# Local attention in groups of 64 queries: 120 score columns a head, one transpose a head, one value product a group

## The chip, the core and the metric

The kernel runs on one core of a Trainium2 chip. A core has a matrix engine (TensorE, PE in the profile, with its weight loads listed apart as PEld), a vector engine (VectorE, DVE), a scalar engine (ScalarE, ACT), a general engine (GpSimd, POOL) and a queue that issues transfers (SyncE, SP). Each engine works through its own instructions in order. SBUF is the working memory with 128 partitions, PSUM the memory that TensorE writes, in eight banks. The metric is the device time of one execution in microseconds (us); lower is better.

## The reference, cut to what matters

Three layers follow each other: an attention, a feed-forward layer, and a mixture of eight experts. Only the attention is touched here. Its shapes are batch 2, 8 heads, 768 positions, 64 numbers a head, all in 32-bit floats:

```
block, window = (32, 16)                      # 24 blocks of 32 keys
k_sum = max of k over each block              # 24 summary keys a head
v_sum = mean of v over each block             # 24 summary values a head
scores_l = scale * q @ k.T, kept only where |query - key| < 16
scores_s = scale * q @ k_sum.T + log(32)
a = softmax over [scores_l, scores_s] together
out = a @ [v, v_sum]
```

So a query sees at most 31 near keys and 24 summary keys. After it come `h = x @ w_in`, `g = h * clip(h+3,0,6) / 6`, `g @ w_out`, the routing of tokens to experts with a cap of 192 each, and per expert `relu(x @ w1) @ w2`.

## The kernel before

Queries are taken in groups of 128 (12 groups `n`, six a batch). A group is worked in two halves `h` of four heads (two pairs `pr`), so the attention has 24 halves. For a half, `front` (L364) computes scores, `soften` (L391) the softmax, `turn` (L406) the transposed weights, and `values` (L416) the product with the values:

- `front`: for each head a matrix product with 64 contraction rows: the 128 queries are stationary (`qT`), and 184 columns move: 160 near keys (128 queries and 16 to each side) and 24 summary keys. `window` (L351) lays these keys out in the tile `kw`: one copy from `kT` (L360) and the summary keys twice (L361, L362), since even heads have the summaries behind the near keys and odd heads in front. Even heads lie on partitions 0 to 63 and odd heads on 64 to 127 of `qT` and `kw` (L371, L372). VectorE then adds the mask and takes the row maximum of each head (L381).
- `soften`: ScalarE takes the exponential with the sum of each row (L397); VectorE the reciprocal (L400); GpSimd multiplies the whole tile `A` (L402). `A` holds two heads in 384 columns, with 16 columns between them that are cleared at the start (L220).
- `turn`: a pair of heads is transposed in three pieces of 128 columns (L411), six a half, and ScalarE copies each pair out of PSUM (L413). The middle piece holds keys of both heads.
- `values`: `VA` holds 128 of the near values, `VB` what is left of them together with the summary values, for two heads side by side. Each head has a product with `VA` into its half of the PSUM partitions (L422, L423); each pair has one more with `VB`, added to it (L425). `load_v` (L163) brings the values with four transfers a group. `vsum_place` (L197) puts the mean values of a batch into `VB` (L203 by TensorE, L208 by VectorE), once a batch.

A matrix product in 32-bit floats is carried out as two matmuls, each with its weight load, so every such source line has twice as many instructions in the trace as in the code. A transpose is one.

The order of work on each engine is that in which the program is written. `drive` (L56) interleaves generators: each says with `yield` what its step is worth, and the one that is furthest behind its due time goes on. The numbers in these `yield`s and the due times (`ATTS`, `END`, `S0`, `S1`) are constants of the program. The first three groups of attention run in `prologue` (L735). The attention of the groups behind runs between the products of the first feed-forward layer, `gemm1` (L571: L581 to L583, twelve matmuls for each `f`, in 384 columns); its `gate` (L595) is on VectorE. Beside the first unit of `gemm1` the 64-bit-packed weights are still converted by VectorE (L275) and split by ScalarE and GpSimd (L292, L293). At most two halves are between `front` and `turn` (`LAG`).

Of the kernel before, what the change touches and what calls it, by code (L numbers as in the profile page):

```python
# [19 lines left out]
E, EF = 8, 1024  # L20
N = B * S
# [4 lines left out]
U = UT * 128  # L26
# [5 lines left out]
SCALE = 1.0 / math.sqrt(D)  # L32
NEG = -1e9 / SCALE
# [51 lines left out]
def build(ctx, tc, q, k, v, w_in, w_out, w_gate, w1, w2, out):  # L85
    nc = tc.nc
    PE, ACT, DVE, POOL, SP = nc.tensor, nc.scalar, nc.vector, nc.gpsimd, nc.sync
# [28 lines left out]
    def bank(i):  # L116
        return psum.tile([128, 512], FT, name=f"bank{i}")
# [3 lines left out]
    early = Arena()  # L121
    conv = Arena()
    sums = Arena()
    ident = consts.tile([128, 128], FT)
# [11 lines left out]
    mask = att.tile([128, 3, NB + 160 + NB], FT)  # L136
    LAG = 2
    Abuf = [att.tile([128, 2, 384], FT, name=f"A{i}") for i in range(LAG + 1)]
    VA = [att.tile([128, HP, 2, D], FT, name=f"VA{i}") for i in range(2)]
    VB = [att.tile([128, HP, 2 * D], FT, name=f"VB{i}") for i in range(2)]  # L140

    def warm(n):

# [17 lines left out]
        raw[kind, b, i] = x  # L161

    def load_v(n):  # L163
        b, i = divmod(n, 6)
        va, vb = VA[n % 2], VB[n % 2]
        i0 = i * 128
        for s in range(2):
            vh = v[b, s:H:2]
            lo = i0 - W if s == 0 else i0 + W
            a, z = max(lo, 0), min(lo + 128, S)  # L170
            SP.dma_start(va[a - lo:z - lo, :, s, :], vh[:, a:z, :].rearrange("h s d -> s h d"))
            lo, row = (i0 + 112, 0) if s == 0 else (i0 - W, 96)
            a, z = max(lo, 0), min(lo + 32, S)
            SP.dma_start(vb[row + a - lo:row + z - lo, :, s * D:(s + 1) * D],
                          vh[:, a:z, :].rearrange("h s d -> s h d"))
# [6 lines left out]
    zones, zi = flat[2][:, :192], flat[3][:, :192].bitcast(I32)  # L182

    def vsum(b, g):
        x, m = vss[g], BLK // 2
# [5 lines left out]
            m //= 2  # L191

    def zone():
        POOL.iota(zi, pattern=[[1, 192]], base=-48, channel_multiplier=-1)
        DVE.tensor_scalar(zones, zi, 0.0, 1.0 / BLK, op0=OP.is_equal, op1=OP.mult)

    def vsum_place(b):  # L197

        p = bank(4)
        for h in range(H):  # L200
            i, s = h % HP, h % 2
            at = 48 + NB * i - (32, 72)[s]
            PE.matmul(p[:, h * D:(h + 1) * D], zones[:, at:at + 128], vm[b][h // HP], start=True, stop=True)  # L203
        pv = p.rearrange("p (h s d) -> p h s d", s=2, d=D)
        for i in range(2):
            for s in range(2):
                r = slice(32 + 32 * s, 64 + 32 * s)
                DVE.tensor_copy(VB[i][r, :, s * D:(s + 1) * D], pv[r, :, s, :])  # L208

    raw["qraw", 0, 0] = q0[0]  # L210
    for g in range(2):
# [5 lines left out]
    for x in VA + VB:  # L217
        POOL.memset(x, 0.0)
    for x in Abuf:
        DVE.memset(x, 0.0)  # L220

    zone()
    band = early.take([160])
    POOL.iota(band, pattern=[[1, 160]], base=-W, channel_multiplier=-1,
              allow_small_or_imprecise_dtypes=True)
    DVE.tensor_tensor(band, band, band, op=OP.mult)
    DVE.memset(mask, math.log(BLK) / SCALE)
    for c in range(3):
        DVE.tensor_scalar(mask[:, c, NB:NB + 160], band, float(W * W), NEG, op0=OP.is_ge, op1=OP.mult)
    DVE.memset(mask[:, 0, NB:NB + W], NEG)  # L230
    DVE.memset(mask[:, 2, NB + 160 - W:NB + 160], NEG)


    WH, WL = {}, {}
# [102 lines left out]
    def q_prep(n, hps=range(HP)):  # L337
        b, i = divmod(n, 6)
        x = raw["qraw", b, i]
        p = bank(7 if n % 2 else 4)  # L340
        a, z = hps[0], hps[-1] + 1
        if a == 0:
            fr[n] = att.tile([128, HP, 128], FT, name="qT"), att.tile([128, HP, NB + 160 + NB], FT, name="kw")
        for hp in hps:
            PE.transpose(p[:, hp * 128:(hp + 1) * 128],
                         x[:, 2 * hp:2 * hp + 2, :].rearrange("p h d -> p (h d)"), ident)
        ACT.activation(fr[n][0][:, a:z], p[:, a * 128:z * 128].rearrange("p (h s) -> p h s", s=128), AF.Copy)
        if n >= UT and (n + 1) % 6:
            soon.append(partial(load_rows, "qraw", q, *divmod(n + 1, 6)))

    def window(n, hps=slice(0, HP)):  # L351
        i = n % 6
        kw = fr[n][1][:, hps]
        a, z = max(i * 128 - W, 0), min(i * 128 + 128 + W, S)
        c = NB + a - (i * 128 - W)
        if i == 0:
            DVE.memset(kw[:, :, NB:c], 0.0)
        if i == 5:
            DVE.memset(kw[:, :, c + z - a:NB + 160], 0.0)
        DVE.tensor_copy(kw[:, :, c:c + z - a], kT[:, hps, a:z])  # L360
        DVE.tensor_copy(kw[:, :, :NB], ks[:, hps])  # L361
        DVE.tensor_copy(kw[:, :, NB + 160:], ks[:, hps])  # L362

    def front(n, h, after):  # L364
        b, i = divmod(n, 6)
        qT, kw = fr[n]
        A = Abuf[(2 * n + h) % (LAG + 1)]
        sp = [bank(0), bank(1)]
        for pr in range(2):
            hp = 2 * h + pr  # L370
            PE.matmul(sp[0][:, pr * 192:pr * 192 + 184], qT[:64, hp, :], kw[:64, hp, NB:], start=True, stop=True)  # L371
            PE.matmul(sp[1][:, pr * 192:pr * 192 + 184], qT[64:, hp, :], kw[64:, hp, :NB + 160], start=True, stop=True)  # L372
        if after:
            q_prep(n + 1)
        mk = mask[:, 0 if i == 0 else 2 if i == 5 else 1]
        sm = att.tile([128, 4, 4], FT, name="sm", bufs=2)
        for pr in range(2):
            for s in range(2):
                o = A[:, pr, 0:184] if s == 0 else A[:, pr, 200:384]
                m = mk[:, NB:] if s == 0 else mk[:, :NB + 160]  # L380
                DVE.tensor_tensor_reduce(out=o, in0=sp[s][:, pr * 192:pr * 192 + 184], in1=m, scale=1.0,  # L381
                                         scalar=-3e38, op0=OP.add, op1=OP.max,
                                         accum_out=sm[:, 0, 2 * pr + s:2 * pr + s + 1])
        DVE.tensor_scalar(sm[:, 1], sm[:, 0], -SCALE, None, op0=OP.mult)
        if after:
            window(n + 1)
        later.append((A, sm))
# [2 lines left out]

    def soften():  # L391
        A, sm = later.pop()
        for pr in range(2):
            for s in range(2):
                o = A[:, pr, 0:184] if s == 0 else A[:, pr, 200:384]
                c = 2 * pr + s
                ACT.activation(o, o, AF.Exp, bias=sm[:, 1, c:c + 1], scale=SCALE, accum_out=sm[:, 2, c:c + 1])  # L397
        yield 1
        DVE.tensor_scalar(sm[:, 2], sm[:, 2], 1e-9, None, op0=OP.add)
        DVE.reciprocal(sm[:, 3], sm[:, 2])  # L400
        Av = A.rearrange("p a (s c) -> p (a s) c", s=2)
        POOL.tensor_tensor(Av, Av, sm[:, 3, :, None].to_broadcast([128, 4, 192]), op=OP.mult)  # L402

    ats = {}

    def turn(n, h):  # L406
        A = Abuf[(2 * n + h) % (LAG + 1)]
        for pr in range(2):
            p = bank(2 + pr)
            for c in range(3):  # L410
                PE.transpose(p[:, c * 128:(c + 1) * 128], A[:, pr, c * 128:(c + 1) * 128], ident)  # L411
            at = att.tile([128, U], FT, name="at", bufs=4)
            ACT.activation(at, p[:, :384], AF.Copy)  # L413
            ats[n, h, pr] = at

    def values(n, h):  # L416
        va, vb = VA[n % 2], VB[n % 2]
        if h == 0:
            xps[n] = bank(4 if n % 2 else 7)
        pair = [(2 * h + pr, ats.pop((n, h, pr)), xps[n][:, (2 * h + pr) * 128:(2 * h + pr + 1) * 128]) for pr in range(2)]  # L420
        for hp, at, o in pair:
            PE.matmul(o[:64], va[:, hp, 0, :], at[:, 0:128], start=hp == 0, stop=False, skip_group_check=True)  # L422
            PE.matmul(o[64:], va[:, hp, 1, :], at[:, 256:384], start=hp == 0, stop=False, skip_group_check=True)  # L423
        for hp, at, o in pair:
            PE.matmul(o, vb[:, hp, :], at[:, 128:256], start=False, stop=True, skip_group_check=True)  # L425
# [786 lines left out]
```

## Time and profile before

| what | value |
|---|---|
| median of 3 runs | 619.5 us (616.31 to 622.27) |
| the profiled execution's own time | 620.14 us |
| its span | 617.9 us |
| granted TensorE clock over the span | 0.981 |
| busy: TensorE, VectorE, ScalarE, GpSimd | 573.1, 413.6, 300.3, 191.0 us |
| TensorE's share of the span | 93% |
| bytes moved by transfers | 74.24 MB |

A row of the profile's list of groups reads: source line, engine, operation, what is written from what, the shape, the count, then the time in which at least one was busy, the mean of one in ns, and the idle time of the engine before it with what ended it. For a matmul, `128*64` is rows by columns of the stationary operand and `128x128` the moving one. The mean of a matmul is longer than the time from its start to the next start, because matmuls are pipelined: what one costs in a row of them is read from the starts in the timeline.

### The profile page before, as it was taken

Reading aid. Unit: us, or ns where it says so; the run is one execution under the profiler, and the core shown is the slowest. Engines: PE = TensorE matmul, PEld = TensorE weight load, DVE = VectorE, ACT = ScalarE, POOL = GpSimd, SP = SyncE. Lnnn points to the kernel's source line nnn. Section 1 sums busy time; section 2 is a strip of 40 time slices with the busy share of each in tenths; the row PEclk is TensorE's granted clock in tenths of the full one; section 3 lists DMA queues with packets and bytes.
Section 4 is the critical chain, followed back from the end, with each engine's and each line's share of the span. In section 5 each row is a group of like instructions: output and inputs, shape, how many; then the busy total and the mean of one; then the engine's idle time right before and its main releaser. Section 6 shows DMA issues by size and latency. Waiting matters only on the chain.

```text
span 617.9 us, 10534 instructions
## 1 busy us (share of the span) xinstructions
PE 573.1 (93%) x3571; PEld 483.5 (78%) x3571; DVE 413.6 (67%) x1197; ACT 300.3 (49%) x718; POOL 191.0 (31%) x212
## 2 busy tenths in 40 slices
PE   6688896999999998889999999999999999999993
PEld 5566775988889997776678787877788889888882
DVE  7878898454454338995003878876568888888880
ACT  3457654454555535554123213232656676767760
POOL 1535556610221104335235445435501011110111
PEclk8789999999999999999999999999999999999997
DMA  9945990211110024440006000000579889888910
GB/s 208 241 110 125 211 271 19 56 36 39 39 40 20 1 70 170 171 137 27 1 1 191 15 2 0 2 1 34 187 222 280 245 250 286 250 241 249 268 62 30
DMA packets 99710, 74.24 MB, mean 120 GB/s; under 512 B 44800, under 2 KB 85760, under 8 KB 99264
## 3 DMA queue, kind: packets, MB, share of 16 engines
q1 hardware_dynamic: 97664, 67.17, 39.3%
q0 software_dynamic: 1984, 6.32, 2.8%
q8 instruction: 30, 0.49, 0.3%
q14 instruction: 32, 0.26, 0.1%
HBM read 66.76 MB, written 6.71 MB: 119 GB/s over the span
## 4 chain that ended last, share of the span: by engine, by line
PE 48%; issue 26%; DVE 15%; POOL 5%; ACT 3%; DMA 2%; SPq 0%; POOLq 0%; ACTq 0%; DVEq 0%
PE bank L581 6%; PE bank L582 6%; PE bank L583 6%; PE bank L699 5%; DVE t L275 5%; PE bank L701 5%; PE bank L700 5%; POOL out_dram L1015 2%; PE bank L371 2%; PE bank L883 2%; POOL xs L630 2%; PE bank L608 2%; PE bank L411 2%; PE bank L425 2%; DVE A L381 1%
## 5 line engine op out<-in xcount | busy, mean ns | idle before, releaser
L581 PE MATMUL bank<-x,wh 128*128 128x384 f32 x256 | 92.4, 361 | 8.1 <-DVE t L596 8.1
L302 DVE TENSOR_TENSOR wl<-t,wh 128x1024 fp32r<-128x1024 f32 x64 | 77.0, 1221 | 20.4 <-ACT wh L301 16.9
L676 ACT ACTIVATE work<-t 128x384 fp32r<-128x384 f32 (+2 forms) x80 | 36.4, 459 | 108.3 <-PE bank L700 107.7
L583 PE MATMUL bank<-x,wl 128*128 128x384 f32 x256 | 86.7, 339 | 0.6 <-POOL wl L293 0.6
L582 PE MATMUL bank<-x,wh 128*128 128x384 f32 x256 | 86.5, 338 | 0.5 <-DVE x L74 0.5
L677 POOL TENSOR_TENSOR tlx<-t,work 128x384 fp32r<-128x384 f32 (+1 forms) x58 | 60.5, 1044 | 81.3 <-ACT work L676 78.2
L584 ACT ACTIVATE t<-bank,three 128x384 f32<-128x384 f32 x64 | 37.1, 580 | 84.5 <-PE bank L583 84.4
L699 PE MATMUL bank<-wh,work 128*128 128x512 f32 x192 | 77.9, 406 | 0.0
L402 POOL TENSOR_TENSOR A<-A,sm 128x768 f32<-128x768 f32 x24 | 35.8, 1490 | 129.9 <-DVE sm L400 107.9
L701 PE MATMUL bank<-wh,tlx 128*128 128x512 f32 x192 | 75.3, 392 | 0.1
L700 PE MATMUL bank<-wl,work 128*128 128x512 f32 x192 | 74.8, 390 | 0.0
L1040 PE MATMUL bank<-x,wh 128*128 128x384 f32 x256 | 73.7, 360 | 0.5 <-DVE x L966 0.5
L301 ACT ACTIVATE wh<-t 128x1024 fp32r<-128x1024 f32 x64 | 65.6, 1048 | 0.0
L1042 PE MATMUL bank<-x,wl 128*128 128x192 f32 x256 | 64.2, 251 | 0.0
L596 DVE SCALAR_TENSOR_TENSOR t<-t,bank 128x384 f32<-128x384 f32 x64 | 34.9, 548 | 42.3 <-ACT t L584 40.8
L1015 POOL DMA_INDIRECT out_dram<-t,idx x16 | 14.9, 930 | 141.6 <-DVE t L1064 136.1
L581 PEld LDWEIGHTS bank<-x,wh 128*128 128x128 f32 x256 | 48.5, 189 | 11.6 <-DVE t L596 6.4
L582 PEld LDWEIGHTS bank<-x,wh 128*128 128x128 f32 x256 | 48.7, 190 | 1.1 <-DVE x L74 1.0
L1042 PEld LDWEIGHTS bank<-x,wl 128*128 128x128 f32 x256 | 48.9, 191 | 0.3
L583 PEld LDWEIGHTS bank<-x,wl 128*128 128x128 f32 x256 | 48.4, 189 | 1.0 <-POOL wl L293 1.0
L1056 PE MATMUL bank<-wh,t 128*128 128x512 f32 x128 | 49.0, 392 | 0.0
L1040 PEld LDWEIGHTS bank<-x,wh 128*128 128x128 f32 x256 | 48.1, 188 | 1.2 <-DVE x L966 0.8
(189 smaller groups left out, 1233.2 us busy)
## 6 DMA issues: line engine op xcount, KB each, us to landing
t<-in_moe_w_dram SPq DMA_DIRECT2D x128, 256.0 KB, 4.6
t<-in_moe_w_in_dram SPq DMA_DIRECT2D x16, 512.0 KB, 4.8
big<-in_moe_w_out_dram SPq DMA_DIRECT2D x16, 512.0 KB, 3.2
t<-in_v_dram SPq DMA_DIRECT2D x4, 768.0 KB, 8.1
VA<-in_v_dram SPq DMA_DIRECT2D x20, 128.0 KB, 2.8
t<-xs SPq DMA_DIRECT2D x8, 258.0 KB, 3.6
raw<-in_q_dram SPq DMA_DIRECT2D x8, 256.0 KB, 3.1
t<-in_k_dram SPq DMA_DIRECT2D x12, 128.0 KB, 3.1
```

Source lines behind the costliest of these rows:

```text
L301: ACT.activation(hi, x, AF.Copy)
L302: DVE.tensor_tensor(lo, x, hi.bitcast(FT), op=OP.subtract)
L581: PE.matmul(p, wh[:, kk, :], xh[:, kk, :], start=kk == 0, stop=False)
L582: PE.matmul(p, wh[:, kk, :], xl[:, kk, :], start=False, stop=False)
L583: PE.matmul(p, wl[:, kk, :], xh[:, kk, :], start=False, stop=kk == KD - 1)
L677: (DVE if placed[0] else POOL).tensor_tensor(ths[i][1], t, ths[i][0].bitcast(FT), op=OP.subtract)
L699: PE.matmul(acc[j], th[:, c], WH[s], start=f == 0, stop=False)
L700: PE.matmul(acc[j], th[:, c], WL[s], start=False, stop=False)
L701: PE.matmul(acc[j], tl[:, c], WH[s], start=False, stop=f == NF - 1)
L1040: PE.matmul(p, a[:, kk, :], xt[:, kk].rearrange("p c s -> p (c s)"), start=kk == 0, stop=False, skip_group_check=True)
L1042: PE.matmul(p[:, :CAP], b[:, kk, :], xt[:, kk, 0, :], start=False, stop=kk == KD - 1, skip_group_check=True)
L1056: PE.matmul(p, x, w, start=m == 0 and i == 0, stop=m == NM - 1 and i == 2)
```

## The change

Queries are still taken in groups of 128, but each group has two sub-groups of 64 (`QG`), and each has its own 96 near keys (`WIN` = 64 and 16 to each side). With the 24 summary keys that is 120 columns (`KEYS`) for every head, in the same order for even and odd heads.

- The scores of a head are two products, one a sub-group: 64 stationary queries on 64 contraction rows, 120 moving columns, written to 64 PSUM partitions of the head's bank. Eight products a half take the place of four.
- Mask, exponential and scaling work on 120 columns a head instead of 184 (192 in the scaling). The tile `A` has no gaps and is not cleared at the start.
- A head's 120 columns are one transpose: four a half instead of six, into one PSUM bank, with one copy out of 120 partitions by 512 instead of two of 128 by 384.
- The values of a sub-group (96 near, 24 summary) lie on 120 partitions of a new tile `VW`, for all eight heads, so each head and sub-group has one product of 120 contraction rows, 64 stationary and 64 moving columns, with nothing added to it afterwards. Eight a half take the place of six. `load_v` has two transfers a group instead of four, of 96 positions and eight heads each (80 at an edge of the sequence). `vsum_place` writes 24 partitions by 512 into each of the four places instead of 32 by 256.
- `window` makes two copies from `kT`, of 96 columns a head pair, instead of one of 160.

Nothing is changed in the `yield`s, due times or in the layers behind.

```diff
+QG = 64
+WIN = QG + 2 * W
+KEYS = WIN + NB
...
-    Abuf = [att.tile([128, 2, 384], FT, name=f"A{i}") for i in range(LAG + 1)]
-    VA = [att.tile([128, HP, 2, D], FT, name=f"VA{i}") for i in range(2)]
-    VB = [att.tile([128, HP, 2 * D], FT, name=f"VB{i}") for i in range(2)]
+    Abuf = [att.tile([128, 4, KEYS], FT, name=f"A{i}") for i in range(LAG + 1)]
+    VW = [att.tile([128, 2, H, D], FT, name=f"VW{i}") for i in range(2)]
...
     def load_v(n):
+        for g in range(2):
+            lo = i * 128 + g * QG - W
+            a, z = max(lo, 0), min(lo + WIN, S)
+            SP.dma_start(VW[n % 2][a - lo:z - lo, g], v[b, :, a:z, :].rearrange("h s d -> s h d"))
...
     def vsum_place(b):
...
-        pv = p.rearrange("p (h s d) -> p h s d", s=2, d=D)
-        for i in range(2):
-            for s in range(2):
-                r = slice(32 + 32 * s, 64 + 32 * s)
-                DVE.tensor_copy(VB[i][r, :, s * D:(s + 1) * D], pv[r, :, s, :])
+        pv = p[WIN:KEYS].rearrange("p (h d) -> p h d", d=D)
+        for x in VW:
+            for g in range(2):
+                DVE.tensor_copy(x[WIN:KEYS, g], pv)
...
-    for x in Abuf:
-        DVE.memset(x, 0.0)
...
     def window(n, hps=slice(0, HP)):
...
+            for g in range(2):
+                lo = i * 128 + g * QG - W
+                DVE.tensor_copy(kw[:, :, g, :WIN], kT[:, hps, lo:lo + WIN])
+        for g in range(2):
+            DVE.tensor_copy(kw[:, :, g, WIN:], ks[:, hps])
...
     def front(n, h, after):
-            PE.matmul(sp[0][:, pr * 192:pr * 192 + 184], qT[:64, hp, :], kw[:64, hp, NB:], start=True, stop=True)
-            PE.matmul(sp[1][:, pr * 192:pr * 192 + 184], qT[64:, hp, :], kw[64:, hp, :NB + 160], start=True, stop=True)
+            for g in range(2):
+                for s in range(2):
+                    r, c = slice(64 * s, 64 * s + 64), slice(QG * g, QG * g + QG)
+                    PE.matmul(sp[s][c, pr * KEYS:(pr + 1) * KEYS], qT[r, hp, c], kw[r, hp, g], start=True, stop=True)
...
     def turn(n, h):
-        for pr in range(2):
-            p = bank(2 + pr)
-            for c in range(3):
-                PE.transpose(p[:, c * 128:(c + 1) * 128], A[:, pr, c * 128:(c + 1) * 128], ident)
-            at = att.tile([128, U], FT, name="at", bufs=4)
-            ACT.activation(at, p[:, :384], AF.Copy)
+        p = bank(2 + h)
+        for c in range(4):
+            PE.transpose(p[:KEYS, c * 128:(c + 1) * 128], A[:, c], ident)
+        at = att.tile([128, 4, 128], FT, name="at", bufs=2)
+        ACT.activation(at[:KEYS], p[:KEYS].rearrange("p (c s) -> p c s", c=4), AF.Copy)
...
     def values(n, h):
-            PE.matmul(o[:64], va[:, hp, 0, :], at[:, 0:128], start=hp == 0, stop=False, skip_group_check=True)
-            PE.matmul(o[64:], va[:, hp, 1, :], at[:, 256:384], start=hp == 0, stop=False, skip_group_check=True)
-        for hp, at, o in pair:
-            PE.matmul(o, vb[:, hp, :], at[:, 128:256], start=False, stop=True, skip_group_check=True)
+        for pr in range(2):
+            hp = 2 * h + pr
+            for g in range(2):
+                at0 = hp * 128 + g * QG
+                for s in range(2):
+                    PE.matmul(xps[n][64 * s:64 * s + 64, at0:at0 + QG], vw[:KEYS, g, 2 * hp + s, :],
+                              at[:KEYS, 2 * pr + s, g * QG:(g + 1) * QG], start=True, stop=True, skip_group_check=True)
```

More of the change, by code (lines that the diff above doesn't have):

```diff
@@ L135, in build @@
     ks = att.tile([128, HP, NB], FT)
[L136 removed]
+    mask = att.tile([128, 3, KEYS], FT)
     LAG = 2
[L138 to L140 removed]
+    Abuf = [att.tile([128, 4, KEYS], FT, name=f"A{i}") for i in range(LAG + 1)]
+    VW = [att.tile([128, 2, H, D], FT, name=f"VW{i}") for i in range(2)]
     def warm(n):
@@ L193, in zone @@
     def zone():
-        POOL.iota(zi, pattern=[[1, 192]], base=-48, channel_multiplier=-1)
+        POOL.iota(zi, pattern=[[1, WIN + 104]], base=-WIN, channel_multiplier=-1)
         DVE.tensor_scalar(zones, zi, 0.0, 1.0 / BLK, op0=OP.is_equal, op1=OP.mult)
@@ L215, in build @@
         SP.dma_start(raw["qraw", 0, 0][:, hs], q[0, hs, :128, :].rearrange("h s d -> s h d"))
-    for x in VA + VB:
+    for x in VW:
         POOL.memset(x, 0.0)
-    for x in Abuf:
-        DVE.memset(x, 0.0)
     zone()
-    band = early.take([160])
-    POOL.iota(band, pattern=[[1, 160]], base=-W, channel_multiplier=-1,
+    band = early.take([WIN])
+    POOL.iota(band, pattern=[[1, WIN]], base=-W, channel_multiplier=-1,
               allow_small_or_imprecise_dtypes=True)
+    DVE.tensor_scalar(band[QG:], band[QG:], float(QG), None, op0=OP.add)
     DVE.tensor_tensor(band, band, band, op=OP.mult)
@@ L228, in build @@
     for c in range(3):
-        DVE.tensor_scalar(mask[:, c, NB:NB + 160], band, float(W * W), NEG, op0=OP.is_ge, op1=OP.mult)
-    DVE.memset(mask[:, 0, NB:NB + W], NEG)
-    DVE.memset(mask[:, 2, NB + 160 - W:NB + 160], NEG)
+        DVE.tensor_scalar(mask[:, c, :WIN], band, float(W * W), NEG, op0=OP.is_ge, op1=OP.mult)
+    DVE.memset(mask[:QG, 0, :W], NEG)
+    DVE.memset(mask[QG:, 2, WIN - W:WIN], NEG)
     WH, WL = {}, {}
@@ L353, in window @@
         kw = fr[n][1][:, hps]
[L354 to L362, printed above, removed]
+        if i in (0, 5):
+            for g in range(2):
+                lo = i * 128 + g * QG - W
+                a, z = max(lo, 0), min(lo + WIN, S)
+                if z - a < WIN:
+                    DVE.memset(kw[:, :, g, :W] if a > lo else kw[:, :, g, WIN - W:WIN], 0.0)
+                DVE.tensor_copy(kw[:, :, g, a - lo:z - lo], kT[:, hps, a:z])
+        else:
+            for g in range(2):
+                lo = i * 128 + g * QG - W
+                DVE.tensor_copy(kw[:, :, g, :WIN], kT[:, hps, lo:lo + WIN])
+        for g in range(2):
+            DVE.tensor_copy(kw[:, :, g, WIN:], ks[:, hps])
     def front(n, h, after):
@@ L378, in front @@
             for s in range(2):
[L379 to L383, printed above, removed]
+                c = 2 * pr + s
+                DVE.tensor_tensor_reduce(out=A[:, c], in0=sp[s][:, pr * KEYS:(pr + 1) * KEYS], in1=mk, scale=1.0,
+                                         scalar=-3e38, op0=OP.add, op1=OP.max, accum_out=sm[:, 0, c:c + 1])
         DVE.tensor_scalar(sm[:, 1], sm[:, 0], -SCALE, None, op0=OP.mult)
@@ L392, in soften @@
         A, sm = later.pop()
-        for pr in range(2):
[L394 to L397, printed above, removed]
+        for c in range(4):
+            ACT.activation(A[:, c], A[:, c], AF.Exp, bias=sm[:, 1, c:c + 1], scale=SCALE, accum_out=sm[:, 2, c:c + 1])
         yield 1
@@ L400, in soften @@
         DVE.reciprocal(sm[:, 3], sm[:, 2])
-        Av = A.rearrange("p a (s c) -> p (a s) c", s=2)
-        POOL.tensor_tensor(Av, Av, sm[:, 3, :, None].to_broadcast([128, 4, 192]), op=OP.mult)
+        POOL.tensor_tensor(A, A, sm[:, 3, :, None].to_broadcast([128, 4, KEYS]), op=OP.mult)
     ats = {}
```

28 lines of the change are left out of this document (8 added, 20 removed).

## The prediction

> **What bounds the kernel now.** I read the table of engine time by stretches first, to find which engine is last in each part of the attention. The profiled execution took 620.14 us (span 617.9), 0.6 above the median of 619.5; I sum against the former and take off 0.6 at the end. Columns: length, then busy time with instruction count of PE, PEld, DVE, ACT, POOL, then granted clock, transfer share, GB/s.
>
> ```profile
> 0.00:55.70 55.70, 41.67 (x281) 32.92 (x282) 44.66 (x149) 27.79 (x87) 21.57 (x26) 0.88 0.74 177
> 55.70:106.00 50.30, 41.36 (x273) 35.73 (x272) 45.93 (x101) 26.99 (x77) 27.44 (x18) 1.00 0.70 168
> 106.00:217.00 111.00, 109.07 (x743) 98.08 (x742) 51.08 (x202) 57.84 (x171) 28.97 (x24) 0.98 0.14 32
> ```
>
> Three stages. **A** (to 55.7, where the first feed-forward matmul starts): nobody is full; a chain through all engines sets it. **B** (to 106): DVE is busy 45.93 of 50.30, PE has 9 us to spare. **C** (to 217): PE is busy 109 of 111, everything else about half. Behind 217 the change touches only the last values product and moves the rest as it is. So matmul time counts in C, VectorE time in B, latency in A.
>
> Next, the timeline of TensorE in C, for what one half costs from start to start (start, length, engine, line).
>
> ```profile
> 148.28 0.32 PE L422 MATMUL bank<-at,VA 128*64 128x128 f32 x1
> 148.29 0.32 PE L423 MATMUL bank<-at,VA 128*64 128x128 f32 x1
> ...
> 148.55 0.27 PE L422 MATMUL bank<-at,VA 128*64 128x128 f32 x1
> ...
> 148.66 0.27 PE L422 MATMUL bank<-at,VA 128*64 128x128 f32 x1
> ...
> 148.87 0.71 PE L425 MATMUL bank<-at,VB 128*128 128x128 f32 x4
> 149.34 0.43 PE L581 MATMUL bank<-x,wh 128*128 128x384 f32 x1
> ...
> 151.53 0.82 PE L411 MATMUL bank<-ident,A 128*128 128x128 f32 x6
> 152.27 0.42 PE L371 MATMUL bank<-kw,qT 64*128 64x184 f32 x1
> 152.28 0.42 PE L372 MATMUL bank<-kw,qT 64*128 64x184 f32 x1
> 152.53 0.32 PE L371 MATMUL bank<-kw,qT 64*128 64x184 f32 x1
> ...
> 152.69 0.32 PE L371 MATMUL bank<-kw,qT 64*128 64x184 f32 x1
> ...
> 153.10 0.44 PE L581 MATMUL bank<-x,wh 128*128 128x384 f32 x1
> ```
>
> Two things to see. Products on different parts of the array start 10 ns apart (L371 with L372 on row halves, L422 with L423 on column halves): they run together. And a row of them advances by its columns: 0.11 us for 128 (148.55 to 148.66), 0.155 to 0.16 for 184. A half costs 0.74 for the transposes, 0.83 for the scores, 1.06 for the values, 2.63 us in all.
>
> **The change on TensorE, per half.** Transposes: six become four; 0.64 of the 0.74 is six times 0.107, the rest the switch to the scores; two fewer save 0.21.
>
> Scores: 0.83 is four passes (two pairs, two passes each in 32-bit) of 0.155, plus 0.21 of switching. Now there are 16 matmuls of 120 columns on four quarters of the array. If the quarters run together, as halves do, four passes of 120/184 x 0.155 = 0.101 remain: 0.61, saving 0.22. If only two run together, eight passes: 1.02, losing 0.19. If none do, sixteen: 1.83, losing 1.00. No row shows quarters of rows and columns at once; the nearest are the halves above and four column strips:
>
> ```profile
> 239.20 0.64 PE L550 MATMUL bank<-x 128*32 128x256 f32 x8 [1.07 <-issue]
> 239.77 0.66 PE L544 MATMUL bank<-ident,x 128*128 128x128 f32 x4
> ...
> 138.54 1.89 PE L203 MATMUL bank<-t 96*128 96x64 f32 x16
> 140.36 0.32 PE L422 MATMUL bank<-at,VA 128*64 128x128 f32 x1
> ...
> 141.38 0.71 PE L425 MATMUL bank<-at,VB 128*128 128x128 f32 x4 [0.36 <-DVE VB L208]
> ...
> 425.96 0.44 PE L917 MATMUL bank<-prop,big 128*128 128x8 f16 x12
> 426.26 0.48 PE L699 MATMUL bank<-wh,work 128*128 128x512 f32 x1
> ```
>
> Eight matmuls of 256 columns on four strips took 0.57; one after another at 0.00084 us a column they would take 1.7. Four at once therefore works, and I take 0.61.
>
> Values: 1.06 is eight passes of 0.107 plus 0.20. Now there are four pairs of column halves, so again eight passes, of 64 columns. By columns a pass is 0.054. From above: L203 has the same 64 moving columns with 128 stationary and took 1.82/16 = 0.114 a matmul, so there the stationary side paced it. Now both sides have 64. I take 0.075, nearer to the lower end because both rows advance by their longer side. One switch fewer: 0.15 in place of 0.20. 8 x 0.075 + 0.15 = 0.75, saving 0.31 (0.48 at 0.054; nothing at 0.114).
>
> The Trainium skill, page "TensorE: Matmul & The Clock Gate", section "LDWEIGHTS (loading the stationary operand)", gives a weight load as its stationary columns over 1.2 per ns, so an estimate of 53 ns for 64. By it a pass would be 0.054 and the total 2.0 us lower than mine, 604; no run here has shown 64 by 64.
>
> So 0.74 a half. The groups of stage C count 72 transposes, 12 halves: 8.9 us. Against it stands the mean-value copy of the second batch (timeline of DVE, and a row of the groups).
>
> ```profile
> L411 PE MATMUL bank<-ident,A 128*128 128x128 f32 x72 | 10.5, 285 | 0.9 <-POOL A L402 0.9
> ...
> 140.47 1.74 DVE L208 COPY VB<-bank 32x256 f32<-32x256 f32 x4 [1.85 <-PE bank L203]
> ...
> L74 DVE TENSOR_TENSOR x<-bank,x 128x512 fp32r<-128x512 f32 x10 | 6.7, 670 | 0.6 <-ACT x L442 0.6
> ```
>
> Before, only L425 waited, for two copies of 0.435. Now every product of that half needs the 24 rows, and two copies are 512 wide. For that I take L74, 0.67 out of the same memory. TensorE starts at 140.47 + 1.34 = 141.81 and ends at 142.56 instead of 141.85, where my sum had 0.31 earlier: 1.0 lost. In the first batch the spacer matmuls behind L203 cover it; without them it would be about as much. **C: 8.9 - 1.0 = 7.9.**
>
> **B, VectorE and GpSimd.** Rows from the groups (busy, mean ns), then the timelines of DVE and POOL.
>
> ```profile
> L402 POOL TENSOR_TENSOR A<-A,sm 128x768 f32<-128x768 f32 x22 | 32.8, 1492 | 116.5 <-DVE sm L400 94.5 <-ACT qT L347 12.0 <-ACT at L413 7.1
> L381 DVE CUSTOM_DVE_ANT_0 A<-bank,mask 128x184 f32<-128x184 f32 x88 | 25.4, 344 | 9.0 <-PE bank L372 7.4 <-PE bank L371 1.3 <-issue 0.3
> L596 DVE SCALAR_TENSOR_TENSOR t<-t,bank 128x384 f32<-128x384 f32 x37 | 20.3, 549 | 26.0 <-ACT t L584 24.6 <-DMA VB<-in_v_dram 1.2
> L360 DVE COPY kw<-kT 128x640 f32<-128x640 f32 x8 | 3.8, 481 | 0.0
> L360 DVE COPY kw<-kT 128x288 f32<-128x288 f32 x2 | 0.5, 272 | 0.0
> ...
> 85.66 1.42 DVE L275 SCALAR_TENSOR_TENSOR t<-t 128x512 int32<-128x512 int32 x2
> ...
> 90.45 1.84 DVE L275 SCALAR_TENSOR_TENSOR t<-t 128x512 int32<-128x512 int32 x1
> ...
> 90.26 1.49 POOL L402 TENSOR_TENSOR A<-A,sm 128x768 f32<-128x768 f32 x1 [4.99 <-DVE sm L400]
> ```
>
> L381 loses 64 of 184 columns; the slope to L596 is (549-344)/200 = 1.02 ns a column, 65 ns each, 0.26 a half. L402 goes from 768 to 480 columns, in proportion 1.49 to 0.93: 0.55 shorter. That counts for VectorE: a conversion normally takes 0.7 (two in 1.42); the one caught behind L402 took 1.84 and ended just after it. Of the five L402 in B four stand so, at 67.95, 79.17, 90.26 and 99.36. The window goes from one copy of 640 to two of 384, 0.33 each by the slope of the two shapes: 0.18 more, once in B. Four score groups: 4 x 0.26 + 4 x 0.55 - 0.18 = 3.1, times 0.91 for the share of time in which VectorE is last: **B: 2.8** (1 if GpSimd's splits move up and catch the conversions instead).
>
> **A, latency.** The DVE, ACT and PE timelines of the start and the chain of waits from 36 to 56 with its shares by line.
>
> ```profile
> 3.23 2.31 DVE L220 MEMSET A<- 128x768 f32 x3
> 8.27 1.27 DVE L316 TENSOR_REDUCE ks<-kT 128x16 f32<-128x512 f32 x2
> ...
> 7.39 0.60 ACT L315 ACTIVATE kT<-bank 128x512 f32<-128x512 f32 x1 [0.62 <-PE bank L312]
> ...
> 10.10 0.39 PE L371 MATMUL bank<-kw,qT 64*128 64x184 f32 x1 [1.53 <-DVE kw L362]
> ...
> by line: DVE A L381 16.6%; ACT A L397 15.7%; DVE t L275 12.0%; POOL A L402 7.4%; issue 6.5%; PE bank L371 5.5%; DVE sm L384 4.8%; PE bank L411 4.4%; PE bank L422 3.9%; ACT at L413 3.8%; PE bank L425 3.3%; SPq L174 3.0%; PE bank L345 2.9%; A
> 37.56 0.17 DVE sm L384
> 41.58 0.53 DVE sm L384
> ```
>
> The clearing of `A` (2.31) goes. L316 then waits for ScalarE instead: its third input is ready at 7.99, so it ends at 8.7 instead of 9.5, and the first scores start 0.75 earlier. From there to 36: two score groups 0.5, L402 0.55, and about 0.7 of TensorE at its lower clock. From 36 to 56 the shares of 20 us give L381 3.3 us, of which 19% goes (0.6); L397 3.1 us, whose 64 of 184 columns I put at a tenth (0.3); L402 once, 0.55; L384, held from 0.17 to 0.53 while L402 runs, about 0.4; the three TensorE steps 0.74; two evictions of `at` become one, 0.2; two windows cost 0.3 more. That is 2.5 and 2.5, 5.0. Such a chain finds other ways, so I take six tenths. **A: 3.0** (1.5 to 5).
>
> Costed at nothing: in C the shorter exponentials and the longer windows (ACT 57.84, DVE 51.08 of 111; if VectorE were last there, windows would cost 0.18 a group), and the value transfers, a fifth more bytes in two issues instead of four on SP's queue, ahead of which only weight and query loads stand. They are issued two groups ahead, over 14 us in C. Transfers take 0.14 of the engines there.
>
> Sum: 3.0 + 2.8 + 7.9 = 13.7. 620.1 - 13.7 - 0.6 = 605.8, **606 us**. Its own bounds: A and B 2.5 to 8.1, C 12 x 0.54 (values at 0.10) - 1 = 5.5 up to 12 x 0.91 - 1 = 9.9: 601 to 611.
>
> **Rivals.** (1) Only two of the four score quarters run at once: 0.41 a half more, 4.9 in C and about 1 in A: 612. For it: no row shows quarters; against it: L550's four strips. 0.14.
>
> (2) The shorter chains of A and B are filled by other waits and only C pays: 620.1 - 7.9 - 0.6 = 612. For it: in A no engine is full. 0.12.
>
> (3) On the other side: TensorE's instruction stream becomes the bound. A half has 26 matmuls before (8, 6, 12) and 36 after (16, 4, 16). No 32-bit block above beats L550's 0.57/8 = 71 ns a matmul. If that is a rate and not its columns, scores cost 16 x 0.071 + 0.21 = 1.35, values 1.29, transposes save 0.21: 0.54 more than now, 6.5 in C, with the copies 7.2; A loses 2 of its 3: 623, slower than before. C gains nothing from 54 ns a matmul on (32 x 0.054 + 0.36 are the 2.10 that transposes, scores and values leave it), and the whole is slower from about 62. Against it: twelve small ones (L917) took 0.30, 25 ns each. 0.08.
>
> The same page of the Trainium skill, section "Step-by-step: what each phase is for", says that TensorE's sequencer, where it decodes in software, spends about 62 ns on each MATMUL. That would be this rival; the 25 ns of L917 disagree.
>
> (4) No two of the quarters run at once: 1.22 a half above my case, 14.6 in C, 2 in A: 622. Against it are both pairs of halves. 0.08.
>
> **How the numbers follow.** My case has 0.58. 601 to 617 holds it, (1) and (2) with their spread; (3), (4) and a little of my own tail are left out. A difference of 1% (6.2 us) is about what a measurement of this kernel tells from none. Faster by more (below 613.3): 0.56 of my case, half or more of (1) and (2): 0.70. Within it: 0.22. Slower: 0.08, the upper ends of (3) and (4).
>
> **What would show it.** In the timeline of C: the four score quarters starting within 50 ns, the block near 0.6; values near 0.75; four transposes in about 0.53; a wait of about 1.4 before the first values of the second batch. In the groups: L402's successor near 0.93, the score reduction near 280 ns. In the stretches: C's end about 8 earlier than B's, B about 3 shorter, the first feed-forward matmul near 52.7. The forecast is wrong if score quarters queue, or if TensorE idles in C.

## The result and the profile after

The changed kernel takes 602.8 us (median of 4 runs, 600.27 to 604.67) against 619.5 us (616.31 to 622.27, 4 runs on the same chip): a ratio of 0.973 with a 95% interval from 0.967 to 0.979. The forecast was 606 us, range 601 to 617. The profiled execution took 603.2 us, with a span of 601.4 and a granted clock of 0.972 (before: 620.14, 617.9, 0.981).

The same three stretches as before the change, from the table of engine time of the changed kernel (length; busy time and instruction count of PE, PEld, DVE, ACT, POOL; granted clock; transfer share; GB/s):

```profile
0.00:55.70 55.70, 41.10 (x394) 33.45 (x395) 41.37 (x166) 27.66 (x91) 19.65 (x26) 0.82 0.86 196
55.70:106.00 50.30, 41.37 (x335) 36.58 (x335) 43.22 (x91) 25.19 (x68) 29.88 (x24) 0.97 0.70 164
106.00:217.00 111.00, 108.62 (x927) 98.88 (x926) 53.64 (x217) 54.90 (x165) 18.90 (x21) 0.98 0.19 47
```

The limits are where they were: TensorE is still busy 108.6 of the 111 us from 106 to 217, though it has 927 matmuls there in place of 743. But the stages now end earlier, so fixed stretches no longer fit them. For the comparison I take the ends from the starts of instructions that both kernels have: A ends at the first feed-forward matmul, B at the start of GpSimd's sum over the second batch's values, C at the first transpose of the product folding that follows the attention. "402 to 433" is the stretch from the last counting matmul of the router to the last matmul of the second product, named by its place in the changed kernel. All in us:

| stage | before | after | difference | forecast |
|---|---|---|---|---|
| A | 55.76 | 50.61 | -5.2 | -3.0 |
| B | 52.36 | 49.56 | -2.8 | -2.8 |
| C | 124.78 | 114.39 | -10.4 | -7.9 |
| fold to the counting | 187.79 | 187.83 | 0.0 | 0 |
| 402 to 433 | 28.97 | 31.05 | +2.1 | 0 |
| the rest | 168.24 | 167.94 | -0.3 | 0 |
| span | 617.9 | 601.4 | -16.5 | -13.7 |

The timeline of TensorE in the changed kernel shows one half in C. Its blocks are read from start to next start:

```profile
138.84 0.69 PE L419 MATMUL bank<-at,VW 120*64 120x64 f32 x16
139.45 0.44 PE L576 MATMUL bank<-x,wh 128*128 128x384 f32 x1
...
141.65 0.60 PE L404 MATMUL bank<-ident,A 128*120 128x128 f32 x4
142.18 0.64 PE L372 MATMUL bank<-kw,qT 64*64 64x120 f32 x16
142.75 0.44 PE L576 MATMUL bank<-x,wh 128*128 128x384 f32 x1
```

Values take 139.45 - 138.84 = 0.61 (before 1.06), transposes 0.53 (0.74), scores 0.57 (0.83). The 16 score matmuls start between 142.18 and 142.56: four within 20 ns, a gap of about 0.1 us, four again. So the four quarters of the array do run together. The same view where the second batch's mean values are placed, and at the start of the kernel:

```profile
9.38 0.64 PE L372 MATMUL bank<-kw,qT 64*64 64x120 f32 x16 [0.47 <-ACT qT L340]
...
19.97 1.12 PE L338 MATMUL bank<-ident,t 128*128 128x128 f32 x4 [4.14 <-DMA t<-in_q_dram]
...
50.61 0.44 PE L576 MATMUL bank<-x,wh 128*128 128x384 f32 x1
...
127.53 1.90 PE L198 MATMUL bank<-t 96*128 96x64 f32 x16
130.26 0.34 PE L419 MATMUL bank<-at,VW 120*64 120x64 f32 x4 [0.83 <-issue]
130.83 0.73 PE L419 MATMUL bank<-at,VW 120*64 120x64 f32 x12 [0.23 <-DVE VW L202]
```

The first scores start 0.72 earlier than before (10.10). At 19.97 there is a wait of 4.14 for the second group's queries which before was 0.16 (at 18.77): the work ahead of it ends 2.8 us earlier, and the transfer, issued at 9.4 in both kernels, lands 1.2 us later, by the ends of these two waits. Behind it SyncE now issues the loads of `w_in` at 13.9 instead of 17.4; whether these hold it up wasn't tested. At 130 TensorE waits 0.83 + 0.23 for the copies of the mean values. The groups of GpSimd and VectorE over the attention (busy, mean ns, idle before):

```profile
L396 POOL TENSOR_TENSOR A<-A,sm 128x480 f32<-128x480 f32 x24 | 24.3, 1011 | 123.4 <-ACT at L406 75.1 <-DVE sm L395 31.4 <-ACT qT L340 11.5
L380 DVE CUSTOM_DVE_ANT_0 A<-bank,mask 128x120 f32<-128x120 f32 x96 | 21.4, 277 | 7.5 <-PE bank L372 7.1 <-PE bank L148 0.3
L202 DVE COPY VW<-bank 24x512 f32<-24x512 f32 x8 | 5.1, 689 | 3.5 <-PE bank L198 3.5
```

The scaling went from 1492 to 1011 ns, the score reduction from 344 to 277, and a copy of the mean values takes 689.

### The profile page after: what moved, and what is told of

It reads as the page before. It is cut to its first block, busy times and chain, and to the rows that moved or that the text cites. A ratio compares the mean times of both kernels' runs of the same rounds, so it can differ in the third digit from the quotient of the medians.

```text
span 601.4 us, 10922 instructions
## 1 busy us (share of the span) xinstructions
PE 554.1 (92%) x3811; PEld 468.0 (78%) x3811; DVE 402.8 (67%) x1208; ACT 288.7 (48%) x694; POOL 179.2 (30%) x210
## 4 chain that ended last, share of the span: by engine, by line
PE 49%; issue 26%; DVE 12%; POOL 5%; ACT 3%; DMA 3%; SPq 1%; POOLq 0%; ACTq 0%; DVEq 0%
PE bank L576 7%; PE bank L577 6%; PE bank L578 6%; PE bank L694 5%; PE bank L696 5%; PE bank L695 5%; DVE t L268 4%; POOL out_dram L1010 2%; PE bank L878 2%; POOL xs L625 2%; PE bank L419 2%; PE bank L603 2%; DMA t<-in_q_dram 2%; PE bank L372 2%; PE bank L539 1%
## 5 line engine op out<-in xcount | busy, mean ns | idle before, releaser
L396 POOL TENSOR_TENSOR A<-A,sm 128x480 f32<-128x480 f32 x24 | 24.3, 1011 | 123.4 <-ACT at L406 75.1
```

## The experiments

Twelve kernels ran, ten edits and twice the changed kernel itself, in three groups. Each group ran on a chip of its own and has its own runs of the kernel before (619.2, 619.8 and 620.9 us), and a ratio is to those. Each edit is one to the changed kernel. The first group is `e1` to `e4`, the second `e5` to `e7`, the third `e8` to `e10`.

**The changed kernel again**, beside the second and the third group, without an edit.

> The changed kernel as it is, as the yardstick beside the next three: 602 to 604, first feed-forward matmul near 50.6, sums of the second batch near 100.2, first products of the last layer near 438.

> The changed kernel again, as it is, beside these: 598 to 603 us, the first feed-forward matmul between 47.8 and 50.6 us as in its two profiles so far, and the granted clock at 0.5 for 5 to 12 us behind the wait for the second query group.

Measured: 597.9 us, 0.970 (0.964 to 0.975), and 602.6 us, 0.972 (0.967 to 0.977), against 0.973 the first time. The first of them lies outside what was expected (602 to 604, first feed-forward matmul near 50.6 and not at 47.78), and the second's first feed-forward matmul, 47.06, is a little earlier than expected. Their profiled executions took 597.1 and 598.8 where the first took 603.2. Where that difference lies is the best measure of what a profile of one execution is worth here, though chips differ too:

| stage | first profile | second | third |
|---|---|---|---|
| A | 50.61 | 47.78 | 47.06 |
| B | 49.56 | 49.67 | 49.82 |
| C | 114.39 | 112.88 | 112.90 |
| 402 to 433 | 31.05 | 28.94 | 31.50 |

In A the granted clock (the third number from the end) tells them apart. The changed kernel's first profile in stretches of 5 us:

```profile
20.00:25.00 5.00, 5.00 (x34) 4.36 (x35) 2.62 (x12) 2.58 (x10) 4.69 (x6) 0.50 1.19 277
25.00:30.00 5.00, 5.00 (x36) 4.78 (x35) 3.72 (x7) 1.62 (x8) 0.14 (x1) 0.50 0.90 210
30.00:35.00 5.00, 4.71 (x66) 3.32 (x62) 3.44 (x18) 2.56 (x9) 0.99 (x1) 0.79 0.88 246
```

And its third:

```profile
20.00:25.00 5.00, 4.76 (x38) 4.12 (x38) 2.14 (x8) 2.58 (x10) 4.69 (x6) 0.61 1.18 271
25.00:30.00 5.00, 4.22 (x56) 3.53 (x56) 4.83 (x14) 2.22 (x9) 0.26 (x1) 1.00 1.05 242
30.00:35.00 5.00, 3.16 (x55) 2.38 (x53) 4.83 (x27) 3.18 (x11) 1.67 (x2) 0.91 1.18 262
```

Behind the same wait of 4.1 to 4.7 us the clock is at half for some 12 us in one execution and for 4 in the other, with 36 and 56 matmuls in the second stretch. Of the nine profiles that have this wait six took the long course (the first profile, the four edits of the first group and `e6_place_early`) and three the short one (both repeats and `e8_value_pair`). The kernel before, in its one profile, was at 0.50 and 0.55 from 25 to 35, so part of the 5.2 of A can be chance of this kind, in either direction. In C it is the same on a smaller scale. The five us from the first values product after the wait at 130, in the first profile and in the third:

```profile
130.26:135.26 5.00, 4.77 (x30) 4.48 (x31) 2.29 (x4) 0.01 (x1) 0.00 (x0) 0.66 0.00 0
```

```profile
126.97:131.97 5.00, 4.76 (x53) 4.20 (x54) 2.85 (x5) 1.52 (x6) 0.00 (x0) 1.00 0.01 3
```

The waits ahead of them are the same (0.83 or 0.84, and 0.23). Once the clock fell and once it did not, and C differs by 1.5 us. Over all profiles that have this wait it fell in six and held in five.

**Clearing put back** (`e1_clear`), three copies of what was taken away:

```diff
+    pad = att.tile([128, 768], FT, name="pad")
+    for _ in range(3):
+        DVE.memset(pad, 0.0)
```

> The changed kernel with three clears of 128 by 768 put back on VectorE where the old kernel cleared A (they clear a spare tile). Theory of the prediction: the clears hold the first key maxima, so the first scores start about 0.75 us later (10.1 instead of 9.4) and the whole takes 0.75 more, 603.5. Rival: the changed kernel's start is paced by the transfer of the second query group, for which TensorE waits 4.1 us until 19.97; then the first scores are 0.75 later, but the first feed-forward matmul stays near 50.6 and the time near 602.8.

Measured: 604.6 us, 0.977 (0.974 to 0.980); the first scores start at 10.35, 0.97 later than in the changed kernel, but the first feed-forward matmul at 51.17, only 0.56 later. Both profiles have the long course of the clock. So of what the clearing cost at the front, at most about half reaches the end of A; 0.56 is little beside the spread of A, and beside `e3_score_order` with the same course (50.99) it is 0.18.

**Scaling at its old width** (`e2_pool768`): `A` has 192 columns a head again, and GpSimd multiplies all 768. Since their gaps must hold numbers, GpSimd clears the three tiles at the start.

```diff
-att.tile([128, 4, KEYS], FT, name=f"A{i}")
+att.tile([128, 4, 192], FT, name=f"A{i}")
...
-    for x in VW:
+    for x in VW + Abuf:
         POOL.memset(x, 0.0)
...
-        POOL.tensor_tensor(A, A, sm[:, 3, :, None].to_broadcast([128, 4, KEYS]), op=OP.mult)
+        POOL.tensor_tensor(A, A, sm[:, 3, :, None].to_broadcast([128, 4, 192]), op=OP.mult)
```

> The changed kernel with GpSimd's scaling back at 768 columns a half (192 a head, of which 72 are unused and cleared once at the start on GpSimd); everything else stays at 120. Theory: VectorE's conversions stand behind the scaling, so its 0.48 us a half count: the scaling takes 1.47 instead of 0.99, stage B (first feed-forward matmul to the sums of the second batch on GpSimd) goes from 49.6 to about 51.5, A loses 0.5 to 1.5, C nothing: 605 to 606. Rival: GpSimd is busy 30% of the span and has room, so nothing moves: 603 within 0.5.

Measured: 607.5 us, 0.982 (0.979 to 0.986). A is 53.50, 2.9 longer than the first profile and 2.5 longer than `e3_score_order`, both with the long course of the clock, though the clearing alone moves the first scores to 10.67, 1.3 later. B is 51.78, 1.8 to 2.2 longer than in `e3_score_order` (50.01) and the three profiles of the changed kernel. C is 113.73, where nothing was expected: with the clock held behind the wait it compares with 112.9 and is 0.8 longer, since transposes there wait 0.96 for GpSimd in place of 0.48, and one feed-forward matmul 0.64 in place of 0.29. In B VectorE's integer conversions show it, first the changed kernel, then this one (groups of 56 to 106 us):

```profile
L396 POOL TENSOR_TENSOR A<-A,sm 128x480 f32<-128x480 f32 x4 | 4.2, 1060 | 15.2 <-DVE sm L395 9.1 <-ACT at L406 3.1 <-ACT wh L285 3.0
L268 DVE SCALAR_TENSOR_TENSOR t<-t 128x512 int32<-128x512 int32 x24 | 22.4, 934 | 0.6
```

```profile
L396 POOL TENSOR_TENSOR A<-A,sm 128x768 f32<-128x768 f32 x5 | 7.6, 1521 | 19.1 <-DVE sm L395 9.7 <-ACT at L406 6.3 <-ACT wh L285 3.0
L268 DVE SCALAR_TENSOR_TENSOR t<-t 128x512 int32<-128x512 int32 x24 | 24.2, 1006 | 0.6
```

The same 24 conversions take 1.8 us more in sum when GpSimd's multiply is wide (this window holds five of them, the other four). So most of what B gained came from GpSimd's shorter scaling, which holds VectorE's conversions up less, as the forecast had it (2.0 of 2.8).

**Order of the score matmuls** (`e3_score_order`): both pairs of one quarter of the array follow each other, in place of a change of quarter with every product.

```diff
-        for pr in range(2):
-            for g in range(2):
-                for s in range(2):
+        for g in range(2):
+            for s in range(2):
...
+                for pr in range(2):
...
```

> The changed kernel with the same score products in another order: the two products of one quarter of the array follow each other, instead of four quarters in turn. Theory: the quarters run together because neighbours in the program lie on different quarters; with neighbours on the same one, about 13 of 16 passes of 0.1 us follow each other, the block goes from 0.57 to about 1.5, C loses 12 x 0.9 = 11 and A 2 to 3: 615 to 617. Rival: TensorE takes products of free quarters ahead of those that wait, so the order does not matter: block 0.57, 603.

Measured: 603.5 us, 0.975 (0.971 to 0.978). The timeline of TensorE:

```profile
149.03 0.66 PE L372 MATMUL bank<-kw,qT 64*64 64x120 f32 x16
149.62 0.66 PE L338 MATMUL bank<-ident,raw 128*128 128x128 f32 x4
```

0.59 against 0.57. Four matmuls in a row on each quarter, and the quarters still start together: the first four starts are 149.030, .044, .057 and .070. The gain of the scores doesn't hang on which of these two orders they are written in.

**Order of the values, all even heads first** (`e4_value_order`): eight matmuls in a row on one half of the columns, then eight on the other.

```diff
-        for pr in range(2):
-            for g in range(2):
-                for s in range(2):
+        for s in range(2):
+            for pr in range(2):
...
+                for g in range(2):
...
```

> The changed kernel with all value products of the left column half first and then those of the right, instead of in pairs. Theory: no pair runs together, so 16 passes of 0.058 instead of 8: the block goes from 0.61 to about 1.07, C loses 5.5 and A about 1: 609 to 610. Rival: the order does not matter: block 0.61, 603. Third: 64-column passes are paced by their weight loads, which two halves share; then a pass alone is cheaper than 0.058 and the block is between 0.61 and 0.9, 603 to 607.

Measured: 607.3 us, 0.981 (0.977 to 0.985) (the changed kernel: 602.8). The timeline:

```profile
145.55 0.97 PE L419 MATMUL bank<-at,VW 120*64 120x64 f32 x16
146.45 0.45 PE L576 MATMUL bank<-x,wh 128*128 128x384 f32 x1
```

0.90, between the first two cases of the expectation and at the upper end of the third. C holds thirteen blocks of values (208 matmuls of L419 between its ends), and thirteen of 0.28 to 0.29 more are 3.7; C is 116.60, and the clock held at 1.00 behind its wait, so the comparison is with 112.9: 3.7. The starts tell how: four matmuls of one half of the columns start alone, then the fifth to eighth with a partner each (145.832 and 145.838 are the first such pair), then the last four alone, about 0.058 from one to the next.

**The same with runs of four** (`e8_value_pair`): the order `pr`, `s`, `g`.

> In the values of each head pair the two sub-groups of an even head come first and then those of the odd head, so a column half of the array is used by two products (four matmuls with their passes) in a row, in place of one. If TensorE takes up a matmul whose part of the array is free ahead of earlier ones that wait, and looks four ahead, the block of values stays at 0.61 us and the stage from the second sums to the fold at 114.4. If it looks no further than the next one, the block falls to where half of the passes overlap, about 0.85 us, and the stage grows by 12 times 0.24, 2.9 us, to about 117.3, near that of the kernel with all even heads first (116.6). If the order of program counts strictly, only every fourth pass overlaps with its neighbour: about 0.95.

Measured: 602.7 us, 0.970 (0.963 to 0.977).

```profile
137.69 0.73 PE L419 MATMUL bank<-at,VW 120*64 120x64 f32 x16
138.35 0.44 PE L576 MATMUL bank<-x,wh 128*128 128x384 f32 x1
```

0.66, and the first two starts are 13 ns apart: four in a row on one part delay the other part's first start hardly at all. C is 115.16, 0.8 above the profile of the changed kernel with the same fall of the clock (114.39); thirteen times 0.05 is 0.65. Of the three cases stated, looking four ahead comes nearest.

**Loads and places in A** (`e5_q_first`, `e6_place_early`, `e7_both`). The first loads the second group's queries ahead of the values for the sums; the second places the sums' products of the second batch right behind the window of the group that opens it, and no longer ahead of its first values; the third does both.

```diff
+    load_rows("qraw", q, 0, 1)
     for g in range(2):
         vsum_load(0, g)
-    load_rows("qraw", q, 0, 1)
```

```diff
                 q_prep(n)
                 window(n)
+                vsum_place(b)
...
-                    vsum_place(b)
...
+                    if b == 0:
...
+                        vsum_place(b)
...
```

> The changed kernel with the transfer of the second query group issued ahead of the two big value loads for the block means. If TensorE's wait of 4.1 us for that transfer at 16 to 20 us is on the path, A gets 1 to 4 us shorter: 599 to 602. Rival: the block means come 1.1 us later in exchange, GpSimd's sums of them (to 24.2) are what the placing of the means waits for, and A gets no shorter or 1 longer: 603 to 604.

> The changed kernel with the block means of the second batch placed right behind the first window of that batch, two half steps earlier than its first values product. If TensorE's wait there (0.83 and 0.23 us idle, and the half-filled block between) was what the prediction booked as 1.0 lost, C gets about 1.2 shorter: 601.5. Rival: VectorE's four copies then stand ahead of the first score maxima of that batch and the wait moves there: 603.

> Both of the last two. If they add up: 598 to 601; if only the placing pays, 601.5; if neither, 603.

Measured: 600.8 us, 0.972 (0.968 to 0.976); 601.6 us, 0.973 (0.968 to 0.977); 602.1 us, 0.974 (0.970 to 0.978), beside 597.9 of the changed kernel on the same chip. None is measurably better. A is 51.10, 52.57 and 51.24, against 47.78 in that kernel's profile. The groups of TensorE in the first 56 us of `e5_q_first` show why:

```profile
L198 PE MATMUL bank<-t 96*128 96x64 f32 x16 | 3.6, 397 | 5.7 <-POOL t L186 3.4 <-DVE t L183 2.3
L338 PE MATMUL bank<-ident,t 128*128 128x128 f32 x16 | 3.2, 320 | 0.0
```

The wait for queries (L338) is gone, and 5.7 us of waits for the sums (L198), whose values now land later, stand in its place. In `e6_place_early` the waits at 130 are gone, but L198 waits 0.72 for ScalarE's `qT` (L340) and a feed-forward matmul 0.48 for VectorE (L593), 1.20 in place of 1.06: C gets no shorter (114.26). The wait moved, as the rival of that run had it, though to other places.

**Filling the waits** (`e9_warm_q`: 36 spare matmuls ahead of the wait for the queries; `e10_warm_sums`: the loads of `e5_q_first` and 24 spare ones ahead of each half of L198).

```diff
         if after:
+            warm(0 if n else 36)
             q_prep(n + 1)
```

> 36 spare matmuls (0.107 us each, 3.9 us) stand on TensorE ahead of the transposes of the second query group, so that the wait of 4.1 us for that group's transfer is filled. Theory: the halved granted clock from 20 to 32 us follows from that idle time, and how long it stays halved is what makes the first stage come out at 47.8 in one run of the same code and 50.6 in another. Then the clock is near 1.00 from 20 to 32, the blocks of scores and transposes there take 0.6 and 0.5 us and not 1.0, and the first feed-forward matmul starts at 47.5 or earlier; the whole gains 2 to 3 us, 597 to 600. Rival: the clock falls for another reason (the load of the engine at that time, or the start of the program), then it is at 0.5 there all the same and the first feed-forward matmul stays between 48 and 51. Other rival: the clock is up but VectorE or the transfers of the values set the stage, then it stays between 47.5 and 50 with a clock of 1.

> The second query group is loaded ahead of the values for the sums, and 24 spare matmuls stand ahead of each half of the products that place the sums, so that neither wait is idle on TensorE. Theory of the clock: near 1.00 from 16 to 33 us, first feed-forward matmul at 47 to 48.5, against 51.1 with the same order of loads and no spare matmuls. Rival: as with the spare matmuls ahead of the queries, no change, 51.

Measured: 604.1 us, 0.972 (0.968 to 0.976), and 608.9 us, 0.982 (0.977 to 0.987). The clock of `e9_warm_q`, and its timeline:

```profile
20.00:25.00 5.00, 5.00 (x46) 4.84 (x44) 1.52 (x1) 0.26 (x1) 4.62 (x5) 1.00 1.09 276
25.00:30.00 5.00, 4.04 (x45) 3.61 (x44) 2.72 (x14) 3.56 (x17) 0.99 (x1) 1.00 1.14 265
```

```profile
15.90 8.30 PE L148 MATMUL bank<-ident 128*128 128x128 f32 x72
24.04 0.60 PE L338 MATMUL bank<-ident,t 128*128 128x128 f32 x4
```

The clock is 1.00 from 15 to 30, and in `e10_warm_sums` from 15 to 40, so the fall does follow the idle time. But my price for the filler was wrong: a spare product is two matmuls, 72 in all, and took 8.1 us where 4.1 were free. From the query transposes to the first feed-forward matmul this kernel takes 51.22 - 24.04 = 27.2 us, the changed kernel 30.6 (first profile), 28.0 and 26.8. So the clock kept up at 20 is worth up to 3.4 against an unlucky execution and nothing against a lucky one (it still fell here for 3.4 us at 32.5, behind other waits), and the overlong filler gave it back. In `e10_warm_sums` the two fillers took 11 us, and A is 52.94 in spite of the full clock. Both expectations (597 to 600 us, and A of 47 to 48.5) were missed. A filler of the right length wasn't run.

## Why the prediction was right, step by step

The time, the sign and the order of the stages came out as forecast. Two of the three terms were too small (A by 2.2, C by 2.5), and a loss that was not in the forecast, 2.1 behind C, came off again: that the time lies within 3 us of the forecast is in part luck.

- **Scores in C (0.61 forecast, 0.57 measured).** The right step: four quarters at once. Rivals (1) and (4), two or one at a time (1.02 and 1.83), are out by the block alone.
- **Values in C (0.75 forecast, 0.61 measured).** This is the mis-sized term. I took 0.075 a pass, between 0.054 by columns and 0.114 by L203. Measured are starts 0.058 apart, and 0.61 = 8 x 0.058 + 0.15. L203 was no near row for it: it had 128 stationary columns, twice as many. The count by columns was the better guide. The Trainium skill, page "TensorE: Matmul & The Clock Gate", section "LDWEIGHTS (loading the stationary operand)", gives a weight load as its stationary columns over 1.2 per ns, an estimate of 53 ns for 64. The measured 58 ns lie nearer to it than to my 75.
- **Transposes (0.53 forecast, 0.53 measured).** So a half saves 0.21 + 0.26 + 0.45 = 0.92, not 0.74; times twelve 11.0 in place of 8.9.
- **The copies of the second batch (1.0 lost).** The forecast was a wait of about 1.4; measured are 0.83 + 0.23 = 1.06, since the first values product waits for one copy only (half of the group's places), where I let it wait for two. The copy's 0.67 was right (689 ns). Not in the forecast: in six of eleven profiles the clock falls behind this wait, which costs 1.5 more. C gained 10.4 with that and 11.9 without, where I had 7.9.
- **The count of halves (12 of everything).** Behind 217 I saw only the last values product, but the kernel before has two of them there (from 217.34 and from 223.40) and a row of transposes (220.57). Between the ends of C lie thirteen blocks of values, and before the change most of a thirteenth row of transposes, at half the clock (1.48 us from 108.03). By the times from start to start without waits, before against the second profile of the changed kernel: transposes 9.61 to 6.07, scores 9.89 to 6.87, values 13.87 to 8.21, and TensorE's waits in C 1.93 to 2.39. That is 11.8 of the 11.9.
- **B (2.8 forecast, 2.8 measured).** The mechanism is shown by the wide scaling (1.8 to 2.2 of the 2.8 go back). The scaling's own size was off: 1011 ns against 930, so that it fell by 0.32 of its time where its columns fell by 0.375; the score reduction came out at 277 against about 280.
- **A (3.0 forecast, 5.2, 8.0 and 8.7 measured).** The steps at its start are right (first scores 0.72 earlier, 0.75 forecast). The factor of six tenths on a raw 5.0 was a guess for waits that take the place of others. One did (4.14 for the queries), and yet all three profiles gained more than the 5 that was my bound. The narrower scaling gives 1.2 to 2.9 of it (`e2_pool768` against the first profile and `e3_score_order`, with and without the 1.3 by which its first scores are late), where my sum had 0.55 twice and 0.4 for L384, before the factor. How much of the rest belongs to the change is not settled, as A differs by 3.6 between executions of the same code, with the clock, and the kernel before has one profile.
- **Behind C (0 forecast).** The first profile lost 2.1 between 402 and 433 again. The timeline of the changed kernel:

```profile
424.62 0.50 PE L694 MATMUL bank<-wh,work 128*128 128x512 f32 x1 [1.45 <-ACT work L671]
426.03 0.51 PE L694 MATMUL bank<-wh,work 128*128 128x512 f32 x1 [0.43 <-ACT work L671]
```

  The code there is the same in both kernels. The second profile of the changed kernel has none of these waits (28.94), the third has (31.50), so they are no fixed consequence of the change. Of the ten edits, too, the three of the second group have none and the other seven have some; the second profile comes from that group, so they go with the group and its chip. What sets them off stays open.
- **Rival (2)**, that only C pays, is out: B paid in full, and A more than I took. **Rival (3)**, an issue rate of 71 ns a matmul, is out too: 16 score matmuls start within 0.38 us, 25 ns from one to the next on average, and TensorE took 927 matmuls through from 106 to 217, as busy as with 743 before.

## What to carry to other kernels

Where a small contraction and a small output leave parts of the array free, more and smaller matmuls can cost less than fewer large ones, if no column is computed that is thrown away afterwards and long runs of instructions don't go to one part: here four in a row cost little, eight in a row cost half of the overlap. Price a pass by the longer of its stationary and moving columns and look for a row with the same count on both sides, not one that shares only one of them. Before a difference of 2 or 3 us in a latency-bound start is put down to an edit, profile the same code again: here it moved by up to 3.6 us, together with the granted clock.

## What the runs showed that I had not expected

- **Matmuls are taken up ahead of others that wait for their part of the array.** With 4 in a row on one part little is lost (scores 0.59 against 0.57, values 0.66 against 0.61); with 8 in a row the other half starts with the fifth (0.90). All of these orders fit a limit of about four waiting matmuls for each part. That is read from the starts; the records don't name the part of the array. So matmuls on different parts do not keep strictly to the order of the program, as TensorE's instructions were said to do at the outset.
- **The clock falls or holds behind the same wait.** After 1.06 us of waits at 130 it was at half for 3.4 us in six profiles (0.66 over the next 5 us) and at 1.00 in five. Behind the wait at 20 (2.3 to 5.8 us) it fell in all nine profiles that have it, for 3.4 to 4.5 us of the work behind the wait or for 12 to 14. In each trace all changes of the granted clock lie whole multiples of 3.41 us apart. Where this grid stands differs between executions, and it tells the eleven apart: in the six the wait of 0.83 us ends before the next point of the grid, in the five the grid cuts it, or it starts there. In the first profile the clock falls at 131.08, behind both waits:

```profile
127.67:131.08 3.41, 2.35 (x29) 2.10 (x29) 1.61 (x3) 0.58 (x1) 0.00 (x0) 1.00 0.00 0
131.08:134.50 3.42, 3.42 (x21) 3.30 (x17) 1.47 (x3) 0.00 (x0) 0.00 (x0) 0.50 0.00 0
```

  That was read off afterwards, and it isn't the idle time of one stretch alone: `a0_after` has the whole 1.06 between two points of the grid, and held. The Trainium skill, page "TensorE: Matmul & The Clock Gate", section "Part 1: The HAM clock gate (the "warmup" mystery)", says that a free-running window of 3413 ns decides it, and that the clock falls after at least one idle window. The grid of 3.41 us agrees with that, but a whole idle window isn't needed by these runs: from its last matmul ahead of the wait to the first one behind it TensorE stood for 0.83 us, and for 0.23 after four more.
- **Earlier isn't sooner at a transfer.** The query load that was hidden to 0.16 us became a wait of 4.14 when the work ahead of it got faster and the load itself landed 1.2 us later, and moving the load ahead put 5.7 us of waits on the values that it had passed.
